# PSUM as one set of eight banks, and small elementwise work given a choice of engine, in a fused attention and channel-mix kernel

## The chip, the cores and the metric

The kernel runs on one core of a Trainium2 chip. The metric is the device time of one execution in microseconds (us). A run is called slow when it is more than 1.5% above the fastest of the same kernel. Experiments of one batch ran on one chip and share the runs of the kernel before. The batches ran on three chips; between batches only ratios are compared.

## The reference

Eight batches, eight heads, 576 positions, head width 64. First comes attention with a feature map whose exponent is shifted by the largest absolute projection of each row, then a channel mix with shifted tokens:

```python
def phi(x):
    proj = np.einsum('bhsd,df->bhsf', x, w_phi)
    proj = proj - np.max(np.abs(proj), axis=-1, keepdims=True)
    return np.concatenate([np.exp(proj), np.exp(-proj)], axis=-1)
q_p, k_p = (phi(q), phi(k))
kv = np.einsum('bhsf,bhsd->bhfd', k_p, v)
num = np.einsum('bhsf,bhfd->bhsd', q_p, kv)
den = np.einsum('bhsf,bhf->bhs', q_p, k_p.sum(axis=2))[..., None] + 1e-06
x = num / den                        # then heads side by side: [8, 576, 512]
# channel mix; x_prev is x shifted by one position
xk = mu_k * x + (1.0 - mu_k) * x_prev
xr = mu_r * x + (1.0 - mu_r) * x_prev
k = np.maximum(xk @ w_k, 0.0)        # 512 -> 1024
v = k * k @ w_v                      # 1024 -> 512
out = 1.0 / (1.0 + np.exp(-(xr @ w_r))) * v
```

## The kernel before

The program is a fixed list of some 1,460 small steps. Each word of the list names a step, after a colon the PSUM place it takes, and after a slash the engine that does it. The steps are recorded in this order, each engine's own among them, and the recording layer puts a semaphore wait wherever two instructions on different engines use the same tile.

```python
ORDER = """
...
xf4/ACT xe4/DVE kc5/ACT h0.0:0 h0.1:1 qb5 rl0.0/ACT rl0.1/ACT sq0.0/ACT vc6/POOL vc7/DVE rk6 qp7:1
...
"""
```

PSUM is cut into three pairs of banks (`P`) and two single banks (`M`). Each use asks the pool for a new tile under the tag of its place:

```python
psum = ctx.enter_context(tc.tile_pool(name="psum", bufs=1, space=bass.MemoryType.PSUM))

def ptile(key, name):
    return psum.tile([128, 2, 512], FP, name=name, tag=f"P{plan.place[key]}")

def motile(key, name):
    return psum.tile([128, 512], FP, name=name, tag=f"M{plan.place[key]}")
```

The matmuls of the channel mix use the singles in turn. A half of `h` goes to one bank while the ReLU (`krelu`) of the other bank is read by ScalarE or VectorE:

```python
def h(fc):
    def f():
        s[fc] = ps = motile(("mo", f"h{b}.{fc}"), "ps_h")
        ...
        for c in range(NDC):
            nc.tensor.matmul(ps, lhsT=wk_bf[:, c, fc * 128:(fc + 1) * 128],
                             rhs=xkt[bp][:, c, m0:m0 + 512], start=(c == 0), stop=(c == NDC - 1))
    return f

def rl(fc):
    def f(eng):
        relu(eng, s["kr", fc], s[fc])
    return f
```

Each maximum is split into a high and a low bf16 part on GpSimd, the two mixes of a channel block are single instructions on VectorE, and GpSimd also issues the input loads:

```python
def mhx():
    nmv = s["nm"].rearrange("p k (a g) -> p k a g", a=2)
    nc.gpsimd.tensor_copy(mhv[:, :, 0], nmv)
    nc.gpsimd.tensor_tensor(mhv[:, :, 1], nmv, mhv[:, :, 0], op=ALU.subtract)
...
def mix(i):
    def f():
        ...
        nc.vector.scalar_tensor_tensor(out=t[:, a, (b % 2) * S:(b % 2 + 1) * S], in0=s["d"],
                                       scalar=mu[:, a:a + 1], in1=xs[:, a, 0:S],
                                       op0=ALU.mult, op1=ALU.add)
    return f
...
def ld(which):
    def f():
        t = get(nat, b, inp, [128, NP, 2 * X], BF, "nat")
        src, o = ((k, 0), (q, X))[which]
        nc.gpsimd.dma_start(out=t[:, a0:a1, o:o + X], in_=heads(src, b, a0, a1))
    return f
```

## Time and profile before

| | before |
|---|---|
| median of 3 runs | 305.4 us (305.16 to 306.32) |
| span of the profiled run | 304.2 us |
| busy: TensorE, VectorE, ScalarE, GpSimd | 278.4, 240.3, 223.3, 127.4 us |
| start of the channel mix of batches 0 to 3 | 51.9, 82.7, 117.4, 153.5 us |
| start-to-start time of TensorE beyond its columns, in gaps over 0.25 us | 24.3 us |

The last row is worked out from the trace: for each pair of neighbouring matmuls, the time between their starts less the time of the first one's columns (at 216 ns for 512 columns, the median in this trace), summed where it is over 250 ns.

A profile line is read from left to right. In the page's map of 40 equal slices each digit is the busy share of a slice in tenths. This is TensorE before:

```profile
PE   6688798999899999969999997999999999999993
```

The start is half empty, there is one dent in the middle, and the rest is 9. In the timeline a line has its start, its length, engine, source line, operation and count; square brackets hold the engine's idle time before it and who ended it. This is the loop of the channel mix before, in the trace's PE view and its VectorE and ScalarE neighbours:

```profile
59.39 1.89 PE L779 MATMUL ps_h<-xk,wk_bf 128*128 128x512 bf16 x8
61.00 0.62 ACT L203 ACTIVATE krelu<-ps_h 128x512 bf16<-128x512 f32 x1
```

Eight matmuls, two halves of `h`, run as one block with no bracket: the second half does not wait for the ReLU of the first.

### The profile page before, as it was taken

To read this page: it belongs to the slowest core of one execution; us is meant where nothing else is said; L and a number is where in the kernel's file an instruction comes from. 1 tells how busy PE (TensorE), PEld (TensorE's weight loads), DVE (VectorE), ACT (ScalarE), POOL (GpSimd) and SP (SyncE) were. 2 spreads that over 40 slices of the span, in tenths; PEclk is the share of its full clock that TensorE was granted. 3 is DMA by queue.
4 is the path that set the end of the run, shared out by engine and by line. 5 is a ranking of instruction groups with operands and counts; after the bars stand their busy time and mean duration, and the time that the engine had idled before them with its cause. 6 is when DMAs were issued, how large, how long until landed. Compare 5 with 4: busy or idle time off the path is not lost.

```text
span 304.2 us, 9054 instructions
## 1 busy us (share of the span) xinstructions
PE 278.4 (92%) x3765; PEld 158.4 (52%) x3813; DVE 240.3 (79%) x369; ACT 223.3 (73%) x408; POOL 127.4 (42%) x261
## 2 busy tenths in 40 slices
PE   6688798999899999969999997999999999999993
PEld 2456465565456655534555654454556655554541
DVE  5776789979978999667978988799869888777331
ACT  3397899998689897855888884898797878923410
POOL 7763533696047346653443714353034403400400
PEclk9999989999999999998999999999999999999999
DMA  8999957399989957996957898913924364233125
GB/s 152 204 209 207 169 83 105 59 194 206 194 174 128 148 124 131 197 200 113 177 110 107 145 125 157 162 47 61 187 60 69 11 93 94 58 74 71 39 58 116
DMA packets 66137, 38.18 MB, mean 126 GB/s; under 512 B 47024, under 2 KB 60720, under 8 KB 66096
## 3 DMA queue, kind: packets, MB, share of 16 engines
q1 hardware_dynamic: 51280, 20.82, 39.4%
q0 software_dynamic: 14672, 16.48, 35.1%
q8 instruction: 30, 0.49, 0.7%
q10 hardware_dynamic: 144, 0.29, 0.3%
q14 instruction: 11, 0.09, 0.1%
HBM read 33.62 MB, written 9.44 MB: 142 GB/s over the span
## 4 chain that ended last, share of the span: by engine, by line
PE 61%; DVE 18%; DMA 7%; ACT 6%; issue 3%; POOL 2%; SPq 1%; DVEq 0%; POOLq 0%
PE ps_v L812 14%; PE ps_h L779 13%; PE ps_r L798 7%; PE ps_nd L656 5%; DMA xs<-x_sc 4%; PE ps_kv L635 4%; DVE nm L565 4%; DVE nm L560 3%; DVE xk L706 2%; PE ps_ve L896 2%; ACT q L620 2%; PE ps_he L866 2%; DVE xr L706 2%; PE ps_q L548 2%; PE ps_k L598 2%
## 5 line engine op out<-in xcount | busy, mean ns | idle before, releaser
L620 ACT ACTIVATE q<-ps_qT 128x512 bf16<-128x512 f32 x128 | 67.1, 622 | 3.0 <-PE ps_qT L612 2.8
L575 ACT ACTIVATE k<-ps_k 128x1024 bf16<-128x1024 f32 x64 | 62.9, 1038 | 5.6 <-PE ps_k L598 4.3
L779 PE MATMUL ps_h<-xk,wk_bf 128*128 128x512 bf16 x237 | 60.8, 379 | 1.3 <-issue 0.3
L812 PE MATMUL ps_v<-wv_bf,kk 128*128 128x512 bf16 x243 | 58.2, 379 | 1.0 <-issue 0.3
L565 DVE TENSOR_REDUCE nm<-ps_q 128x8 f32<-128x1024 f32 x32 | 38.7, 1218 | 4.3 <-PE ps_q L548 4.1
L560 DVE TENSOR_REDUCE nm<-ps_k 128x8 f32<-128x1024 f32 x32 | 38.8, 1217 | 3.8 <-PE ps_k L548 3.8
L812 PEld LDWEIGHTS <-kk 128*128 128x128 bf16 x256 | 23.9, 98 | 28.8 <-issue 1.9
L211 POOL TENSOR_TENSOR kk<-krelu 128x512 bf16<-128x512 bf16 x23 | 23.9, 1047 | 35.4 <-DVE krelu L205 21.7
L779 PEld LDWEIGHTS <-wk_bf 128*128 128x128 bf16 x256 | 22.5, 97 | 25.2 <-issue 2.3
L584 POOL CAST mhl<-nm 128x16 bf16<-128x16 f32 x32 | 8.0, 250 | 64.1 <-DVE nm L560 64.0
L798 PE MATMUL ps_r<-wr_bf,xr 128*128 128x512 bf16 x118 | 32.9, 394 | 1.2 <-issue 0.5
L804 ACT ACTIVATE rt<-ps_r 128x512 bf16<-128x512 f32 x32 | 19.5, 609 | 18.0 <-PE ps_r L798 15.7
L700 POOL TENSOR_TENSOR diff<-xs 128x576 bf16<-128x576 bf16 x21 | 28.0, 1336 | 7.6 <-DVE xs L682 2.8
L203 ACT ACTIVATE krelu<-ps_h 128x512 bf16<-128x512 f32 x39 | 23.2, 611 | 10.1 <-PE ps_h L779 8.3
L706 DVE SCALAR_TENSOR_TENSOR xk<-diff,mu_k_t,xs 128x576 bf16<-128x576 bf16 x32 | 28.5, 892 | 1.3 <-POOL diff L700 1.0
L818 DVE SCALAR_TENSOR_TENSOR ob<-rt,ps_v 128x512 f32<-128x512 bf16 x32 | 21.8, 682 | 8.7 <-PE ps_v L812 4.2
L666 DVE TENSOR_TENSOR x_sc<-ps_nd,rden 128x640 bf16<-128x640 f32 x32 | 26.4, 825 | 1.1
L706 DVE SCALAR_TENSOR_TENSOR xr<-diff,mu_r_t,xs 128x576 bf16<-128x576 bf16 x32 | 26.9, 840 | 0.0
L548 PEld LDWEIGHTS <-qkT 64*128 64x128 bf16 x512 | 17.6, 94 | 12.0 <-issue 9.7
L635 PE MATMUL ps_kv<-v,k 64*128 64x65 bf16 x1024 | 22.8, 192 | 0.6 <-ACT q L620 0.4
L635 PEld LDWEIGHTS <-k 64*128 64x128 bf16 x1024 | 19.9, 95 | 5.1 <-issue 3.8
L205 DVE TENSOR_SCALAR krelu<-ps_h 128x512 bf16<-128x512 f32 x25 | 17.1, 688 | 6.6 <-PE ps_h L779 6.0
(99 smaller groups left out, 467.5 us busy)
## 6 DMA issues: line engine op xcount, KB each, us to landing
out_dram<-ob SPq DMA_DIRECT2D x72, 128.0 KB, 2.4
nat<-in_k_dram POOLq DMA_DIRECT2D x6, 576.0 KB, 8.6
nat<-in_q_dram POOLq DMA_DIRECT2D x6, 576.0 KB, 8.9
vt<-in_v_dram POOLq DMA_DIRECT2D x6, 576.0 KB, 9.6
wk_bf<-in_moe_w_k_dram POOLq DMA_DIRECT2D x2, 512.0 KB, 10.8
wv_bf<-in_moe_w_v_dram POOLq DMA_DIRECT2D x2, 512.0 KB, 12.3
nat<-in_k_dram POOLq DMA_DIRECT2D x3, 288.0 KB, 7.4
nat<-in_q_dram POOLq DMA_DIRECT2D x3, 288.0 KB, 7.3
```

What stands on the lines that cost most here:

```text
L211: (nc.vector if eng == "DVE" else nc.gpsimd).tensor_tensor(out_, in_, in_, op=ALU.mult)
L560: nc.vector.tensor_reduce(s["nm"][:, 0, :], s["k"].rearrange("p a (g f) -> p (a g) f", f=128), axis=AX.X, op=ALU.max, apply_absolute_value ...
L565: nc.vector.tensor_reduce(s["nm"][:, 1, :], s["q"].rearrange("p a (g f) -> p (a g) f", f=128), axis=AX.X, op=ALU.max, apply_absolute_value ...
L575: nc.scalar.activation(s[f"k{pn}"], s["k"].rearrange("p a (g f) -> p (a g) f", f=128), AF.Exp, scale=(1.0 if pn == 0 else -1.0))
L620: nc.scalar.activation(t[:, h, :].rearrange("f (g a p) -> f g a p", g=4, a=2), s["qT"].rearrange("f a (g h p) -> f h g a p", g=4, h=2)[:, ...
L635: nc.tensor.matmul(ps[:, hh, pn * 65:(pn + 1) * 65], lhsT=s[f"k{pn}"][r, c, :], rhs=vb[r, a, 2 * g + par, :], start=(pn == 0 and c == 0), ...
L666: nc.vector.tensor_tensor(s["x"].rearrange("p (b s) d -> p b s d", b=2), ndv[:, :, :, 0:64], s["rd"].to_broadcast([128, 2, 5, 64]), op=ALU ...
L700: (nc.vector if eng == "DVE" else nc.gpsimd).tensor_tensor(s["d"], xs[:, a, 64:64 + S], xs[:, a, 0:S], op=ALU.subtract)
L706: nc.vector.scalar_tensor_tensor(out=t[:, a, (b % 2) * S:(b % 2 + 1) * S], in0=s["d"], scalar=mu[:, a:a + 1], in1=xs[:, a, 0:S], op0=ALU.m ...
L779: nc.tensor.matmul(ps, lhsT=wk_bf[:, c, fc * 128:(fc + 1) * 128], rhs=xkt[bp][:, c, m0:m0 + 512], start=(c == 0), stop=(c == NDC - 1))
L798: nc.tensor.matmul(ps, lhsT=xrt[bp][:, c, m0 + ci * 128:m0 + (ci + 1) * 128], rhs=wr_bf[:, c, :], start=(c == 0), stop=(c == NDC - 1))
L812: nc.tensor.matmul(ps, lhsT=s["kk"][:, fc, ci * 128:(ci + 1) * 128], rhs=wv_bf[:, fc, :], start=(fc == 0), stop=(fc == NFC - 1))
```

## The change

The intent: let any step take any of the eight banks, as a pair or single, so that a fourth pair may be in flight; let an edge tile (the positions beyond 512) use the second bank of its own pair in place of two singles; and let mixes and splits of maxima run on GpSimd or VectorE. The whole list of steps was made anew for this, with 26 of 32 pair splits and 8 of 10 edge splits on VectorE, and 31 of 64 mixes on GpSimd. The core of the diff, with the new list and repetitions cut:

```diff
+    def pick(eng):
+        return nc.vector if eng == "DVE" else nc.gpsimd
...
+    banks = [psum.tile([128, 2, 512], FP, name=f"banks{i}") for i in range(4)]
+
     def fill(n, i):
-        t = psum.tile([128, 512], FP, name="ps_f", tag=f"M{i}")
         for _ in range(n):
-            nc.tensor.matmul(t, lhsT=ones[:, 0:128], rhs=ones, start=True, stop=True)
-    def ptile(key, name):
-        return psum.tile([128, 2, 512], FP, name=name, tag=f"P{plan.place[key]}")
-    def motile(key, name):
-        return psum.tile([128, 512], FP, name=name, tag=f"M{plan.place[key]}")
+            nc.tensor.matmul(banks[i // 2][:, i % 2, :], lhsT=ones[:, 0:128], rhs=ones, start=True, stop=True)
+    def ptile(key):
+        return banks[plan.place[key] // 2]
+    def motile(key):
+        i = plan.place[key]
+        return banks[i // 2][:, i % 2, :]
...
         def mte():
-            s["pm"] = pm = motile(("mo", "m" + tag), "ps_me")
-            nc.tensor.transpose(pm[:, 0:64].bitcast(BF), mh, ident)
+            nc.tensor.transpose(s["ps"][:, 1, 0:64].bitcast(BF), mh, ident)
...
-        def mhx():
+        def mhx(eng):
             nmv = s["nm"].rearrange("p k (a g) -> p k a g", a=2)
-            nc.gpsimd.tensor_copy(mhv[:, :, 0], nmv)
-            nc.gpsimd.tensor_tensor(mhv[:, :, 1], nmv, mhv[:, :, 0], op=ALU.subtract)
+            pick(eng).tensor_copy(mhv[:, :, 0], nmv)
+            pick(eng).tensor_tensor(mhv[:, :, 1], nmv, mhv[:, :, 0], op=ALU.subtract)
...
         def mix(i):
-            def f():
+            def f(eng):
...
+                if eng == "DVE":
+                    nc.vector.scalar_tensor_tensor(out=out_, in0=s["d"], scalar=mu[:, a:a + 1], in1=prev,
+                                                   op0=ALU.mult, op1=ALU.add)
+                else:
+                    md = small.tile([128, S], FP, name="md", bufs=2)
+                    nc.gpsimd.tensor_scalar(md, s["d"], mu[:, a:a + 1], None, op0=ALU.mult)
+                    nc.gpsimd.tensor_tensor(out_, md, prev, op=ALU.add)
```

## The prediction

> **What bounds the kernel now.** I read the shares first, then the stretches, then TensorE's waits, then the timeline of the worst hole. The page's first part:
>
> ```profile
> PE 278.4 (92%) x3765; PEld 158.4 (52%) x3813; DVE 240.3 (79%) x369; ACT 223.3 (73%) x408; POOL 127.4 (42%) x261
> ```
>
> TensorE is the fullest engine, but VectorE and ScalarE are near it, so a small delay on any of the three shows. Modelled ends make 278 too much, so I counted TensorE's real work. From the chain of waits, full-speed pieces: 4 matmuls of 512 columns take 0.86 to 0.87 us, 8 take 1.73, the 20 of one ps_nd 0.64, one ps_he half 0.89; likewise about 2.36 us for all seven groups of one head pair. Sum: channel mix 64x0.865 + 32x0.865 + 32x1.73 + edges 17.5 = 156; pairs 32x2.36 = 75.5; first transposes and edge tiles 15. That is **246 us** plus 39 filler matmuls. The other 58 us of the 304.2 us span are where anything can be won. Where they lie, by stretches cut at the first ps_h of each batch (51.9, 82.7, 117.4, 153.5, ... us; columns as the view heads them: PE, PEld, DVE, ACT, POOL busy, clock, DMA share, GB/s):
>
> ```profile
> 0.00:52.00 52.00, 40.60 (x674) 25.83 (x680) 38.96 (x75) 38.03 (x74) 28.60 (x64) 0.97 1.00 164
> 83.00:117.00 34.00, 33.42 (x537) 20.51 (x544) 30.98 (x44) 28.93 (x54) 16.48 (x36) 1.00 0.96 149
> 117.00:153.50 36.50, 33.18 (x448) 17.77 (x448) 28.62 (x39) 25.89 (x45) 18.73 (x36) 0.95 0.99 162
> 220.00:251.00 31.00, 30.74 (x470) 18.28 (x474) 25.46 (x41) 25.39 (x46) 10.01 (x21) 1.00 0.41 57
> 276.70:304.20 27.50, 22.43 (x124) 10.80 (x124) 9.26 (x16) 7.71 (x13) 3.18 (x3) 0.97 0.36 77
> ```
>
> The start takes 52 us for some 22 us of useful TensorE work: about 30 lost. The last matmul ends near 299.3; 4.9 us are the last eviction and store. In between, 247.4 us hold 224 us of work: 23 lost. So three pots: **30 (start), 23 (middle), 5 (end)**. What TensorE waits for by name:
>
> ```profile
> PE ps_me L476 <- POOL mhlt L471: 3.5, 3, 2.4
> PE ps_m L589 <- DVE ob L818: 1.6, 1, 1.6
> PE ps_e L455 <- ACT qkT L197: 1.4, 1, 1.4
> PE ps_q L548 <- ACT qkT L197: 1.4, 2, 1.0
> PE ps_k L548 <- DVE nm L565: 1.2, 4, 0.3
> PE ps_m L589 <- POOL mhl L585: 1.0, 3, 0.4
> ```
>
> The transposes of the maxima (ps_m, ps_me) head the list: they wait for GpSimd's split of each maximum into two bf16 parts. The longest hole in the timeline shows why GpSimd is late:
>
> ```profile
> 131.54 0.23 POOL L199 COPY xs<-xs 128x63 bf16<-128x63 bf16 x1 [2.80 <-DMA xs<-x_sc]
> ...
> 133.37 0.70 POOL L471 TENSOR_TENSOR mhlt<-me,mhlt 128x4 bf16<-128x4 f32 x1
> ...
> 134.53 0.23 PE L476 MATMUL ps_me<-ident,mhlt 128*128 128x128 bf16 x1 [2.44 <-POOL mhlt L471]
> ...
> 138.55 0.23 POOL L199 COPY xs<-xs 128x63 bf16<-128x63 bf16 x1 [2.48 <-DMA xs<-x_sc]
> ...
> 139.31 0.23 PE L589 MATMUL ps_m<-ident,mhl 128*128 128x128 bf16 x1 [0.27 <-POOL mhl L585]
> ```
>
> GpSimd, which takes its work in order, waits for a DMA transpose[...] (the chain puts 13.4 us on it); the tiny splits stand behind that copy, and TensorE stands behind the splits. Start-to-start gaps of TensorE over 250 ns sum to 3.9 us in 130 to 140, and 12 us in all after 50 us.
>
> [...] 1.6 us of ps_m waits for ps_v's eviction (they share one bank) and 1.2 us of ps_k for the reduction that empties ps_q. [...] the difference of 576 columns has a mean of 1336 ns on GpSimd and 495 on VectorE, 2.7x. [...] the mixes have a median of 814 ns, but one took 1900.
>
> **The change part by part.**
>
> *Order.* The whole order is new: 1462 entries, every bank and engine chosen again; filler falls from 39 to 22. What precedes the first ps_h hardly changes: 7 kp, 5 nd. I multiplied the entries of each order by the durations above. Up to the mix that releases the first channel mix (xb3): VectorE 42.9 before, 43.7 after; ScalarE 39.9 and 40.4; TensorE 22.4 and 23.4. After the last ps_nd (nd31) both have the same 31 us of matmuls. Hence neither end becomes shorter by having less work.
>
> *Maximum splits.* 26 of 32 pairs and 8 of 10 edges move to VectorE. GpSimd loses 26x0.487 + 8x0.85 = 19.5 us. VectorE gains, with small VectorE operations of 0.14 to 0.17 us as a guide (an estimate), 26x0.3 + 8x0.56 = 12.3. The split now follows its reduction on the same engine. In the hole above all splits concerned are on VectorE, and the waiting GpSimd copies have no matmul behind them.
>
> *Mixes.* 15 xa and 16 xb move to GpSimd as two instructions (multiply into f32, then add). Estimate: like its one-input copy, 0.74, plus like its difference, 1.34: 2.1 us each, +65 us; VectorE loses 31x0.87 = 27.
>
> *Squares and copies.* ScalarE takes 13 more squares (+8) and gives up 14 copies of kv and mT (-4.5); GpSimd loses 7 squares (-7) and 5 v copies (-4). With the rest: VectorE about 228, ScalarE 229, GpSimd 162 us. Balanced, and none over TensorE. More overlap with GpSimd stretches VectorE: today some 0.08 us for each two-input operation, if doubled over the 100 left about +8. The relief is then about 5 us of 240: not where the gain is.
>
> *Banks.* A fourth pair may be in flight, and an edge tile takes one pair instead of a pair and two singles. In the built programs TensorE's waits fall from 531 to 420; waits on its own engine, which came with handing a tile over, fall from 102 to 1. VectorE's rise from 295 to 381.
>
> *Sum.* Middle: 3.9 us of the hole goes; of the other 8 us of gaps I give 3 to the banks and the shorter path of the maxima. Start: a fourth pair and splits without the trip over GpSimd take 2 of the 30, since the work before xb3 is unchanged (filler there fills idle time, so 17 fewer give nothing). End: 0. Together -9: 305.4 - 9 = **296.5 us**.
>
> **The rivals.**
> 1. *Same holes elsewhere* (300 to 306). The lost middle time is DMA transposes late among loads; a new order meets them at another place. For it: DMA share is near 1 up to 150 us, and every batch still needs its transposes. Against: the matmuls behind are no longer tied to GpSimd.
> 2. *GpSimd[...] becomes the bound* (303 to 310). A chain transpose, copy, difference, two mixes on GpSimd lasts 0.35+1.3+4.2 = 5.9 us against 2.5 on VectorE; four pairs make 23 us of the 31 us of a batch[...]. For it: the 1900 ns mix. Against: only half the mixes move, and the last batch mixes on VectorE.
> 3. *The freedom does more* (285 to 292). A fourth pair lets ScalarE and VectorE, each idle 13 to 14 us in the start, run ahead; the start falls to 46 and the middle loses 12 instead of 23.
>
> **Range and chances.** The floor is 22 + 224 + 5 plus a start that data and ScalarE's 40 us do not let go under about 45, so about 275 to 280; today is 304. I put the centre at one third of the way, 296.5, the range from rival 3 to the mild form of rival 1: 289 to 304. Faster by over 2% means under 299.3. The centre is 3 us below that: chance 0.66; same 0.31; slower, which needs rival 2 in full, 0.03.
>
> **What would show it.** Right: first ps_h at 49 to 51 us; no TensorE gap above 2 us; ps_m and ps_me waiting on GpSimd for under 1 us; VectorE busy 225 to 240, ScalarE 225 to 235, GpSimd 155 to 175; a GpSimd mix of about 2.1 us in all; middle loss near 16. Wrong: a GpSimd wait ahead of ps_h (late mixes), mixes or splits on VectorE stretched well beyond 0.9 and 0.3 us, or a new hole of several us with the clock falling to 0.83[...].

## The result

The changed kernel is correct and takes 361.7 us (median of 4, 360.5 to 363.4) against 305.4 us (305.2 to 306.3) beside it. A ratio in this document is the mean time of one kernel's fast runs over that of the kernel before in the same rounds, so not quite the ratio of the medians quoted; here it is 1.184, 95% interval 1.179 to 1.189. It is **slower by 18%**, and the prediction of 296.5 us was wrong.

The part on shares in the page after, and TensorE's slices:

```profile
PE 288.8 (81%) x3796; PEld 162.4 (45%) x3796; DVE 240.7 (67%) x432; ACT 230.7 (64%) x411; POOL 191.8 (53%) x226
...
PE   7867689878778968687887786897977998989893
```

TensorE, VectorE and ScalarE have within 4% of the work that they had, and their shares have fallen by 9 to 12 points; GpSimd has more work, but stands idle for nearly half of the span. Nobody became the bound; all wait more. TensorE's 9s are gone from one end to the other, so the loss is not one hole. By stretches from one batch's channel mix to the next (the columns are stretch, length, busy time of PE, PEld, DVE, ACT and POOL with their instructions, clock, DMA share, GB/s), first before, batches 0 and 1, then after:

```profile
51.90:82.70 30.80, 29.38 (x383) 16.31 (x385) 27.39 (x40) 26.17 (x49) 17.67 (x29) 1.00 0.95 153
82.70:117.40 34.70, 34.12 (x546) 20.82 (x550) 31.45 (x45) 29.19 (x55) 16.88 (x36) 1.00 0.95 150
```

```profile
54.30:89.10 34.80, 28.86 (x379) 15.56 (x377) 26.52 (x48) 25.07 (x48) 19.79 (x15) 1.00 0.49 85
89.10:141.90 52.80, 42.09 (x594) 24.47 (x592) 34.28 (x60) 33.87 (x60) 30.32 (x35) 0.94 0.77 127
```

The first channel mix starts only 2.5 us later than before (54.4 against 51.9); the loss comes after it, 4 us in batch 0, 18 in batch 1 and some 30 in the later ones. TensorE's gaps over 0.25 us sum to 80.0 us, 55.7 more than before, which is the whole loss of 56 us. The granted clock is lower too, 0.971 in the mean of this run against 0.986; an estimate of the time lost to it, (1 - clock) x span, is 10.4 us against 4.2, so at most some 6 us of the loss can be that. TensorE's waits by name (line that waited, who ended it, us in total, times, longest), the first of them:

```profile
PE banks L792 <- DVE krelu L212: 7.6, 9, 1.5
PE banks L792 <- ACT krelu L210: 7.3, 6, 2.7
PE banks L597 <- DVE mhl L593: 4.7, 4, 2.5
```

L792 is the first matmul of the channel mix. Before, it had 1.3 us of idle time ahead of it in the whole run. Now it waits for ReLUs, and the timeline shows which. The list of steps puts three halves of `h` at banks 6, 7 and 6 (`h0.5:6 h0.6:7 h0.7:6`), with their ReLUs on VectorE, ScalarE and ScalarE:

```profile
65.50 0.68 DVE L212 TENSOR_SCALAR krelu<-banks 128x512 bf16<-128x512 f32 x1
66.23 1.02 PE L792 MATMUL banks<-xk,wk_bf 128*128 128x512 bf16 x4 [0.82 <-DVE krelu L212]
67.29 0.60 ACT L210 ACTIVATE krelu<-banks 128x512 bf16<-128x512 f32 x1 [0.47 <-PE banks L792]
67.94 1.02 PE L792 MATMUL banks<-xk,wk_bf 128*128 128x512 bf16 x4 [0.69 <-ACT krelu L210]
```

The matmuls of 66.23 go to bank 7, and wait until VectorE has read bank 6. Those of 67.94 go to bank 6, which has been free since 66.18, and wait until ScalarE has read bank 7. Matmul and reader take turns where before they overlapped. Banks 6 and 7 are one tile.

I then went through the waits of the built programs and looked, for each, at what the instruction that waits and the one waited for have in common. **False waits**, where the two touch the same tile but different banks or parts of it, number 9 before and 172 after: 87 of TensorE on a reader, 32 of a reader on TensorE, the rest of readers on readers. (These are counts of the program as it was built, not of the trace.) The trace names some of the last kind too:

```profile
DVE krelu L212 <- ACT krelu L210: 7.6, 5, 2.9
ACT rt L817 <- DVE ob L831: 7.0, 3, 4.9
```

The other two costs that the prediction put numbers on were also larger. First GpSimd by shapes after (shapes, count, busy us, mean ns, then the idle time), then VectorE's splits:

```profile
L720 POOL TENSOR_SCALAR md<-diff,mu_r_t 128x576 f32<-128x576 bf16 x16 | 28.8, 1801 | 10.2 <-DVE diff L708 10.0
L721 POOL TENSOR_TENSOR xr<-md,xs 128x576 bf16<-128x576 f32 x16 | 20.6, 1290 | 1.3
```

```profile
L593 DVE TENSOR_TENSOR mhl<-nm,mhl 128x16 bf16<-128x16 f32 x26 | 9.4, 361 | 0.9
L592 DVE CAST mhl<-nm 128x16 bf16<-128x16 f32 x26 | 8.1, 312 | 0.9
```

A mix on GpSimd takes 1.8 + 1.3 = 3.1 us, not 2.1, and a split on VectorE 0.67 us, not 0.3.

### The profile page after: what moved, and what is told of

Its sections match the earlier page's. It is cut to its first block, busy times and chain, and to the rows that moved or that the text cites. A ratio compares the mean times of both kernels' runs of the same rounds, so it can differ in the third digit from the quotient of the medians.

```text
span 358.7 us, 9134 instructions
## 1 busy us (share of the span) xinstructions
PE 288.8 (81%) x3796; PEld 162.4 (45%) x3796; DVE 240.7 (67%) x432; ACT 230.7 (64%) x411; POOL 191.8 (53%) x226
## 4 chain that ended last, share of the span: by engine, by line
PE 47%; DVE 24%; ACT 18%; issue 5%; DMA 2%; POOL 2%; SPq 0%; DVEq 0%; ACTq 0%; POOLq 0%
PE banks L825 13%; PE banks L792 11%; PE banks L811 6%; ACT krelu L210 5%; DVE krelu L212 4%; ACT q L628 3%; DVE ob L831 3%; DVE nm L568 3%; DVE nm L573 3%; ACT rt L817 3%; ACT k L583 2%; PE banks L664 2%; PE banks L879 2%; PE banks L643 2%; PE banks L556 2%
## 5 line engine op out<-in xcount | busy, mean ns | idle before, releaser
L792 PE MATMUL banks<-xk,wk_bf 128*128 128x512 bf16 x256 | 64.0, 384 | 18.7 <-DVE krelu L212 7.6
L628 ACT ACTIVATE q<-banks 128x512 bf16<-128x512 f32 x128 | 66.4, 608 | 12.5 <-PE banks L620 12.4
L583 ACT ACTIVATE k<-banks 128x1024 bf16<-128x1024 f32 x64 | 62.5, 1031 | 10.4 <-PE banks L606 10.1
L825 PE MATMUL banks<-wv_bf,kk 128*128 128x512 bf16 x256 | 59.9, 379 | 4.5 <-ACT rt L817 3.0
L792 PEld LDWEIGHTS <-wk_bf 128*128 128x128 bf16 x256 | 24.0, 98 | 47.5 <-issue 24.1
L573 DVE TENSOR_REDUCE nm<-banks 128x8 f32<-128x1024 f32 x32 | 38.7, 1219 | 9.5 <-PE banks L556 9.5
L568 DVE TENSOR_REDUCE nm<-banks 128x8 f32<-128x1024 f32 x32 | 39.0, 1219 | 5.5 <-PE banks L556 4.6
L811 PE MATMUL banks<-wr_bf,xr 128*128 128x512 bf16 x128 | 33.4, 389 | 9.8 <-ACT krelu L210 3.9
L720 POOL TENSOR_SCALAR md<-diff,mu_r_t 128x576 f32<-128x576 bf16 x16 | 28.8, 1801 | 10.2 <-DVE diff L708 10.0
L556 PE MATMUL banks<-wph,qkT 64*128 64x128 bf16 x512 | 25.9, 224 | 4.7 <-DVE x_sc L674 3.0
L720 POOL TENSOR_SCALAR md<-diff,mu_k_t 128x576 f32<-128x576 bf16 x15 | 26.4, 1762 | 5.4 <-DVE diff L708 4.3
L674 DVE TENSOR_TENSOR x_sc<-banks,rden 128x640 bf16<-128x640 f32 x32 | 26.4, 825 | 1.1
L556 PEld LDWEIGHTS <-qkT 64*128 64x128 bf16 x512 | 18.0, 98 | 12.3 <-issue 10.2
```

The lines of the kernel that those rows point to most:

```text
L556: nc.tensor.matmul(ps[:, par, g * 128:(g + 1) * 128], lhsT=qkT[b][r, g0 + gg + g, :], rhs=wph[r, :], start=(g == 0), stop=(g == 3))
L568: nc.vector.tensor_reduce(s["nm"][:, 0, :], s["k"].rearrange("p a (g f) -> p (a g) f", f=128), axis=AX.X, op=ALU.max, apply_absolute_value ...
L573: nc.vector.tensor_reduce(s["nm"][:, 1, :], s["q"].rearrange("p a (g f) -> p (a g) f", f=128), axis=AX.X, op=ALU.max, apply_absolute_value ...
L583: nc.scalar.activation(s[f"k{pn}"], s["k"].rearrange("p a (g f) -> p (a g) f", f=128), AF.Exp, scale=(1.0 if pn == 0 else -1.0))
L628: nc.scalar.activation(t[:, h, :].rearrange("f (g a p) -> f g a p", g=4, a=2), s["qT"].rearrange("f a (g h p) -> f h g a p", g=4, h=2)[:, ...
L720: nc.gpsimd.tensor_scalar(md, s["d"], mu[:, a:a + 1], None, op0=ALU.mult)
```

## The experiments

The theory (A): the halves of one tile are ordered as if they were one buffer, and this alone serializes TensorE with the readers. The rivals: (B, C) the mixes on GpSimd, by their own time or by stretching VectorE's operations beside them (before, one of VectorE's mixes took 1900 ns beside GpSimd's difference and copy, where the median is 814); (D) static tiles in place of tiles handed out per use; (E, F) the new order of steps itself.

### 1. The false waits, taken away and put in

**a_nodep**: the changed kernel, with every ordering declared absent where two instructions on different engines touch different banks of a tile and have no other tile in common.

```diff
+    def split_banks(new):
+        for b in new:
+            ob = others(b)                         # tiles other than banks
+            for m, bk in banks_of(b).items():      # tile -> banks touched
+                for a, abk, aob in hist.setdefault(m, []):
+                    if a.engine != b.engine and not (bk & abk) and not (ob & aob):
+                        tc.declare_no_dep(b, a, reason="other bank")
+                hist[m].append((b, bk, ob))
```

> The changed kernel, same order, same instructions, same banks; only the dependencies between two instructions of different engines that touch different banks of one two-bank PSUM tile (and share nothing else) are declared absent. Theory A (the two halves of one tile are ordered as if they were one buffer: in the built program 87 waits of TensorE on a reader of the other bank, 32 of readers on a writer of the other bank, 51 of readers on readers): 290 to 305 us, near the 296.5 of the prediction, and no TensorE wait for a krelu ahead of ps_h. Rival B (mixes on GpSimd, 3.06 us each where 2.1 were assumed) and rival C (the new order is simply worse): 345 to 362 us, unchanged.

Measured: 323.1 us (median of 4, 319.1 to 328.0), against 306.7 beside it. Two of the four runs were slow by the rule above, so there is no interval; its two fast runs give a ratio of 320.4 / 306.5 = 1.045. The false waits in the built program fall from 172 to 4, and the waits of L792 on ReLUs leave the head of the list. So A accounts for some 14 of the 18 points, about 42 us on fast runs (38.5 on all). My range of 290 to 305 was missed by 18 us all the same: something else costs 14 to 17 us. TensorE's first two waits now:

```profile
PE banks L597 <- DVE mhl L593: 10.2, 9, 3.4
PE banks L556 <- DVE x_sc L674: 5.5, 2, 5.0
```

**n_peonly**: the same, with only the false waits of TensorE taken away.

```diff
-                    if a.engine != b.engine and not (bk & abk) and not (ob & aob):
+                    if a.engine != b.engine and "PE" in str(b.engine) and not (bk & abk) and not (ob & aob):
```

> The changed kernel with only TensorE's 87 false waits taken away, and the false waits of VectorE, ScalarE and GpSimd on the other half of a tile left in. Theory A-PE (TensorE's own waits on readers of the other half are what costs): 320 to 332 us, nearly all of the 38.5 us. Rival A-readers (the readers that queue behind one another are as much to blame, and TensorE then waits for the late reader of its own bank): 338 to 358 us.

Measured: 332.5 us, ratio 1.085 [1.078, 1.092], a hair above the expected range. TensorE's own 87 false waits are 9.9 of the 13.9 points; those of the readers are the other 4, in this order of taking them away; the readers' alone were not taken away.

**b_shared**: the other direction. The kernel before, its order and engines unchanged, with the two singles as halves of one tile. **b_split**: the same static tiles, but the two singles are two tiles.

```diff
+    ptiles = [psum.tile([128, 2, 512], FP, name=f"ppair{i}") for i in range(3)]
+    mpair = psum.tile([128, 2, 512], FP, name="mpair")        # b_split: two tiles [128, 512]
+    mtiles = [mpair[:, i, :] for i in range(2)]
     def ptile(key, name):
-        return psum.tile([128, 2, 512], FP, name=name, tag=f"P{plan.place[key]}")
+        return ptiles[plan.place[key]]
     def motile(key, name):
-        return psum.tile([128, 512], FP, name=name, tag=f"M{plan.place[key]}")
+        return mtiles[plan.place[key]]
```

> The kernel before with its own order, engines and banks; the three pairs and the two single banks become tiles that live for the whole kernel, and the two single banks are the halves of one tile, as in the changed kernel. Theory A: the false waits alone make it slow, 330 to 370 us, with TensorE waiting for krelu and rt of the other single bank. Rivals B and C: nothing that they name has changed, 304 to 308 us.

> As b_shared, but the two single banks are two tiles. Separates the shared tile from the fact that tiles live for the whole kernel and are no longer handed over by a pool. Theory A: 303 to 309 us, as before. If tiles that live for the whole kernel are themselves the cost: near b_shared.

Measured: b_shared 401.6 us, ratio 1.309 [1.303, 1.315]; b_split 306.4 us, ratio 0.999 [0.995, 1.004]. One shared tile costs 95 us in the order made for two, more than I had expected and more than the change itself; static tiles cost nothing, and D is out. TensorE's waits in b_shared are again those on readers of the other half:

```profile
PE mpair L781 <- ACT krelu L203: 8.1, 11, 1.4
PE mpair L781 <- DVE krelu L205: 6.6, 8, 1.9
```

The built programs hold the sharpest lesson. Counting TensorE's waits whose other side I could tell: 518 before, 417 in b_split, **385 in b_shared** and 393 in the changed kernel. The kernel with the fewest waits is the slowest of the four.

**bs_nodep**: b_shared with the false waits between its halves declared absent (the edit of a_nodep on `mpair`).

> The kernel before with its two single banks as halves of one tile (which took 401.6 us), and now the orderings between instructions that touch different halves declared absent. Theory A (the 95 us were nothing but false waits between the two halves): back to the time before, 304 to 309 us. Rival D (sharing a tile costs by something else too, such as the way its address is formed or the waits are placed): it stays above 315 us.

Measured: 306.1 us, ratio 0.998 [0.993, 1.002]. All 95 us were false waits. The shared tile costs nothing else.

### 2. The mixes on GpSimd

**a_dvemix**: the changed kernel with its 31 mixes back on VectorE. **n_dvemix**: the same on top of a_nodep.

```diff
-tp1.0:4 qt3:0 qa3 nd2:6 rt1.0 mhe1.0/DVE mte1.0+1@2 mce1.0/ACT kp4:2 xb0/POOL qb3 rd2 qte1.0 eqe1.0
+tp1.0:4 qt3:0 qa3 nd2:6 rt1.0 mhe1.0/DVE mte1.0+1@2 mce1.0/ACT kp4:2 xb0/DVE qb3 rd2 qte1.0 eqe1.0
...
```

> The changed kernel with all 31 mixes of GpSimd back on VectorE, same order and banks. Theory A: VectorE gets 27 us more work but is not the bound, 352 to 368 us. Rival B (GpSimd mixes are the cost): 310 to 330 us. Rival C: 355 to 365 us.

> a_nodep (false waits gone, 323 us) with all 31 GpSimd mixes back on VectorE, same order. Theory A2 (of the 17 us that a_nodep is still over before, most comes from the mixes on GpSimd: 3.0 us each, and VectorE's maximum splits standing behind them, up to 1.27 us for an operation that takes 0.17 alone): 302 to 312 us, mhl operations on VectorE with a mean under 0.25 us, TensorE's wait for mhl on VectorE under 5 us. Theory C2 (the order itself is worse): 318 to 332 us, because VectorE gains 27 us of work in an order that was not made for it.

Measured: a_dvemix 367.2 us, ratio 1.196 [1.190, 1.202]: with the false waits in place the mixes are not the cause, and moving them back makes it slightly worse. n_dvemix 314.3 us, ratio 1.023 [1.014, 1.033] (one of its runs was slow): without the false waits the mixes are worth about 2 points, some 7 us. Neither of the expected ranges, 302 to 312 and 318 to 332, was hit; the truth lies between.

How the mixes cost time is seen in a_nodep. The timeline at 79 us, lines of other steps left out:

```profile
79.50 1.27 POOL L721 TENSOR_TENSOR xk<-md,xs 128x576 bf16<-128x576 f32 x1
79.57 1.23 DVE L593 TENSOR_TENSOR mhl<-nm,mhl 128x16 bf16<-128x16 f32 x1
...
80.86 0.23 PE L597 MATMUL banks<-ident,mhl 128*128 128x128 bf16 x1 [3.39 <-DVE mhl L593]
```

The low part of the maximum, 16 columns, takes 1.23 us and ends with GpSimd's addition beside it (at 80.80 and 80.77 us), and TensorE stands behind it. Over the whole of a_nodep the same operation has (minimum, median, maximum in ns):

```profile
L593 DVE TENSOR_TENSOR mhl<-nm,mhl x26: 174/176/1267, 13.0 to 274.9; 128x16 bf16<-128x16 f32 x26
```

The maximum is about the length of GpSimd's addition (1271 to 1297 ns). In n_dvemix the maximum falls to 702 ns, and TensorE's waits for this line from 10.2 to 4.5 us.

**n_mdbf**: a_nodep with the product of a mix kept in bf16, to see why the multiply takes 1.72 us rather than the 0.74 of a copy.

```diff
-                    md = small.tile([128, S], FP, name="md", bufs=2)
+                    md = small.tile([128, S], BF, name="md", bufs=2)
```

> The changed kernel without its false waits (323.1 us), with the product of each mix kept in bf16 rather than f32 on the way. Theory C1 (GpSimd's multiply takes 1.72 us because it writes 4-byte results): the multiply falls below 1.2 us, GpSimd's busy time by over 12 us, and the time to 314 to 320 us. Theory C2 (the multiply costs the same whatever it writes): 1.7 us and 321 to 326 us as before. Precision only is lost by it.

Measured: 319.9 us, ratio 1.043 [1.037, 1.049], as a_nodep's fast runs (so the time alone, just inside C1's range, says nothing for C1). The multiply did not get shorter, and the output type is not the reason:

```profile
L720 POOL TENSOR_SCALAR md<-diff,mu_r_t 128x576 bf16<-128x576 bf16 x16 | 29.0, 1811 | 1.4 <-DVE diff L708 1.2
```

### 3. The splits of maxima

**n_poolmh**: a_nodep with all splits back on GpSimd. **n_both**: with splits on GpSimd and mixes on VectorE, so with the engines of the kernel before.

```diff
-rq0 pb1/ACT eqe0.0 kp0:0 ekt0.0 pa1/ACT rk0 lv1.0.d:0 mh0/DVE pt2:2+3@2 pa2/ACT wr.1.d:0 pb2/DVE tr2
+rq0 pb1/ACT eqe0.0 kp0:0 ekt0.0 pa1/ACT rk0 lv1.0.d:0 mh0/POOL pt2:2+3@2 pa2/ACT wr.1.d:0 pb2/DVE tr2
...
```

> a_nodep with the 26 pair splits and 8 edge splits back on GpSimd, mixes stay on GpSimd. If it is the splits' place on VectorE (blocked by GpSimd) that costs, this is faster than 323: 310 to 318. If GpSimd's queue is the trouble (mixes of 3 us ahead of a split in order), it is slower: 325 to 345 us, TensorE waiting for mhl on GpSimd for over 20 us. I expect the latter.

> a_nodep with splits back on GpSimd and mixes back on VectorE: the engines of the kernel before in the order and on the banks of the changed one. Against n_dvemix it gives the worth of the split's move without GpSimd mixes. If the splits gain on VectorE: n_dvemix is 3 to 6 us faster than this. Expected 305 to 318 us.

Measured, as ratios, with the false waits gone in all four:

| | mixes partly on GpSimd | all mixes on VectorE |
|---|---|---|
| most splits on VectorE | 1.045 (a_nodep, 2 fast runs) | 1.023 (n_dvemix) |
| all splits on GpSimd | 1.184 (n_poolmh, 363.3 us) | 1.116 (n_both, 342.9 us) |

Both runs were slower than I expected (325 to 345, and 305 to 318). The order was made for splits on VectorE, where a split follows its reduction; on GpSimd it queues, behind mixes of 3 us or behind loads (n_both's longest wait, 7.7 us at 18 us, ends with a split that stands behind eight loads issued from 7.8 to 17.4 us). TensorE's waits in n_poolmh:

```profile
PE banks L597 <- POOL mhl L593: 36.5, 14, 8.5
PE banks L485 <- POOL mhlt L481: 17.9, 5, 7.7
```

n_both is the clearest sign that **an order does not carry over to other engines**: its engines for splits and mixes are those of the kernel before, it has no false waits, and it is 11.6% slower.

**b_dvemh**: the kernel before with all splits on VectorE, order unchanged.

```diff
-            nc.gpsimd.tensor_copy(mhv[:, :, 0], nmv)
-            nc.gpsimd.tensor_tensor(mhv[:, :, 1], nmv, mhv[:, :, 0], op=ALU.subtract)
+            nc.vector.tensor_copy(mhv[:, :, 0], nmv)
+            nc.vector.tensor_tensor(mhv[:, :, 1], nmv, mhv[:, :, 0], op=ALU.subtract)
```

> The kernel before with all maximum splits (pairs and edges) on VectorE, nothing else changed. The prediction gave the hole at 130 to 140 us (3.9 us) and part of 3 us more to this part. If so: 299 to 303 us, no gap of TensorE over 2 us near 131 us. If the splits merely wait elsewhere (behind other VectorE work, or blocked by GpSimd): 304 to 309 us.

Measured: 318.1 us, ratio 1.037 [1.030, 1.044], against both expectations. The hole at 131 us is gone, but in the place of one long wait on GpSimd there are many short ones on VectorE:

```profile
PE ps_m L589 <- DVE mhl L585: 6.4, 10, 1.7
PE ps_me L476 <- DVE mhlt L471: 3.1, 6, 0.9
```

These two come to 9.5 us, against 4.5 us on the same lines and GpSimd before; the rest of the 11.3 us is not named.

**b_hole**: the kernel before, with only the three splits of that hole on VectorE.

```diff
-tp4.0:0 kv15:1 kc15/ACT h2.6:0 sq2.4/ACT rl2.5/DVE rt4.0 mhe4.0 rl2.6/DVE nd14:1 rd14 h2.7:1 qb15
+tp4.0:0 kv15:1 kc15/ACT h2.6:0 sq2.4/ACT rl2.5/DVE rt4.0 mhe4.0/DVE rl2.6/DVE nd14:1 rd14 h2.7:1 qb15
...
```

(and `mh16/DVE`, `mh17/DVE` in the next lines)

> The kernel before with just three of its splits of maxima (the 16th and 17th of the main rows and the extra one of the fourth batch, those of the hole at 130 to 140 us) on VectorE in place of GpSimd. My predicted step (the hole is worth 3.9 us, and comes from these splits standing behind other work on GpSimd): 301.5 to 304 us. Rival (the next wait comes soon after it, or the later buffers set the pace anyway): 304.5 to 306.5 us.

Measured: 303.95 us against 306.4, ratio 0.991 [0.988, 0.995] in 5 rounds. This is the one version that **beats both kernels**, by 0.9% or 2.7 us; the interval leaves out 1. The stretch of the hole, before and then in b_hole:

```profile
125.00:145.00 20.00, 16.91 (x220) 8.69 (x222) 14.72 (x21) 12.53 (x22) 11.03 (x24) 0.91 1.02 158
```

```profile
125.00:145.00 20.00, 17.50 (x237) 9.29 (x231) 18.19 (x31) 14.23 (x25) 10.62 (x19) 1.00 1.05 175
```

TensorE is busy longer, the clock stays at 1.00 where it was 0.91, and more gets done (237 matmuls against 220). The gaps in 130 to 140 us fall from 3.9 to 2.8 us; the largest, 1.67 us, now ends with a ReLU on ScalarE. That is 1.1 us of the 2.7. The clock differs as well, over all fast runs of the batch: 0.994 in the mean against 0.987, and (1 - clock) x span, again an estimate, falls from 3.9 to 1.9 us. Whether the shorter hole brought the better clock is not shown.

### 4. What is left of the new order

With the false waits gone 4.5 points stay. **n_norar** takes away from a_nodep also the orderings between two engines that only read one bank; **n_close** does that to n_dvemix, so that all three suspects are gone; **n_load** moves in n_close five input loads ahead of two squarings that GpSimd stands before.

```diff
-                    if a.engine != b.engine and not (bk & abk) and not (ob & aob):
+                    if a.engine != b.engine and not (ob & aob) and (not (bk & abk) or (rd and ard)):
```

```diff
-vc8/DVE r0.0:7 th0.0 ka7 rl0.5/DVE nd6:4 ea7 eb7 rd6 h0.6:7 rl0.6/ACT sq0.4/POOL h0.7:6 rl0.7/ACT
+vc8/DVE r0.0:7 th0.0 ka7 rl0.5/DVE nd6:4 ea7 eb7 rd6 h0.6:7 rl0.6/ACT lk3.0 lq3.0 lv3.0 sq0.4/POOL h0.7:6 rl0.7/ACT
...
```

(with `lk3.0 lq3.0 lv3.0` taken out of their later places, and `lk4.0 lq4.0` moved ahead of `sq1.0/POOL` in the same way)

> The changed kernel without its false waits (323.1 us), and now also without the orderings between two engines that both only read one bank. Theory A3 (readers queue behind readers of the same bank, and this is part of the 17 us still missing): 312 to 319 us. Rival (only the mixes on GpSimd and the order are left as causes): 320 to 326 us.

> The changed kernel without its false waits, without the orderings between two readers of one bank, and with its 31 mixes on VectorE: all three causes taken away at once. If they add up (38.5 + 9 + 5.6 us off 361.7): 306 to 311 us, and nothing is left for the new order itself. Rival (the new order, made for other loads, costs by itself): 312 us or more.

> The kernel with all three causes taken away (314.9 us), with five input loads (third and fourth batch) moved ahead of the two squarings that GpSimd stands before. Theory E (the new order's late loads are what is left): 306 to 311 us, and the third batch's feed-forward starts at 117 to 121 us in place of 125.8. Rival F (the loads are early enough, and what is left is spread over the order of VectorE's and TensorE's work): 313 to 317 us.

Measured: n_norar 317.5 us, ratio 1.031 [1.024, 1.038]; n_close 314.9 us, 1.030 [1.024, 1.035]; n_load 312.9 us, 1.021 [1.017, 1.026].

n_norar looks like 1.4 points less than a_nodep's two fast runs, but n_close is no better than n_dvemix (1.023). The two don't add up, and I call the waits among readers **inconclusive**. The waits concerned are between readers of successive uses of a bank. These three kernels are for measurement and no version to keep: what happens when ScalarE and VectorE read one bank at the same time, no run here shows. In a_nodep, n_norar and n_close I laid the bank of each of the 362 reads of ScalarE and 258 of VectorE beside its times in the trace, and no two overlapped on a bank. Against a cost of such waits speaks b_split: its built program has 180 waits between ScalarE and VectorE where before has 123, at a ratio of 0.999; but that is the old order. The kernels a_nodep, n_dvemix and bs_nodep keep every ordering within a bank.

The expectation that n_close would return to 306 to 311 us failed. Its trace showed why loads are late. GpSimd in n_close, its two squarings and the loads of K and V of batch 3, then the same two loads before:

```profile
62.72 1.04 POOL L218 TENSOR_TENSOR kk<-krelu 128x512 bf16<-128x512 bf16 x1 [18.23 <-DVE krelu L212]
63.70 0.81 POOL L326 DMA_DIRECT2D nat<-in_k_dram  x1
...
85.08 1.63 POOL L218 TENSOR_TENSOR kk<-krelu 128x512 bf16<-128x512 bf16 x1 [11.44 <-ACT krelu L210]
86.66 0.81 POOL L331 DMA_DIRECT2D vt<-in_v_dram  x1
```

```profile
61.59 0.79 POOL L316 DMA_DIRECT2D nat<-in_k_dram  x1
...
63.10 0.76 POOL L321 DMA_DIRECT2D vt<-in_v_dram  x1
```

(Batches are counted from 0: the "third and fourth batch" of the expectation are 3 and 4, and the channel mix that starts at 125.8 us is that of batch 2.) GpSimd takes its queue in order, and a squaring that waits 18.2 us for its ReLU holds up the loads behind it. The first load is only 2 us later than before; V of batch 3 and the two loads of batch 4 behind it are some 24 us later. In one slice of n_close the transfers are at 2 GB/s. n_load issues the first of the five at 43.3 us rather than 63.7 and V of batch 3 at 53.4 rather than 86.7, and gains 2.0 us on the medians, though the two intervals just meet. The channel mix of batch 2 starts at 124.3 us in place of 125.8, not at the 117 to 121 that theory E asked for. So E is a part at most, as far as this run tests it: the loads of batch 4 are still at 73.5 and 74.3 us where before has 63.8 and 64.6, and one slice is still at 2 GB/s. The last 2.1 points, some 6.5 us, are spread: TensorE's gaps sum to 37.5 us in n_load against 24.3 before, no wait by name is over 3.8 us in total, and **their cause stays open**.

## Why the prediction was wrong

**The step that failed is "Banks".** It read the built programs: TensorE's waits fall from 531 to 420, those on its own engine from 102 to 1, a fourth pair may be in flight; and it entered this as a gain inside the 3 us given to "the banks and the shorter path of the maxima". What the runs showed in its place:

- The waits that vanished were worth nothing. b_split removes the same 101 handover waits and has a ratio of 0.999.
- Behind the falling count stood 172 waits of a new kind, between banks that have nothing to do with each other. They cost about 42 us of 56. a_nodep shows it by taking them away, b_shared by putting 220 of them into the kernel before, and bs_nodep by taking those away again.
- The diff held the cause in plain sight: `banks[i // 2][:, i % 2, :]` in place of a tile for each bank. I read the change as eight free banks. In its tiles it is four buffers of two banks.
- I saw that VectorE's waits rise from 295 to 381 and did not ask on what. Counted in the built programs by what they wait for, those on VectorE itself rise from 54 to 135, and those on ScalarE, which hold the readers' false waits, from 54 to 97.

**Two terms of the sum were mis-sized, and they close the busy times.** The mix on GpSimd was set at 2.1 us and is 3.1: the multiply is 1.8 us where I took a copy's 0.74. For 31 mixes 95 us in place of 65, and GpSimd is at 191.8 us where I said 162. A split on VectorE was set at 0.3 us and is 0.67 in the mean. Its two operations have medians of 175 and 176 ns, but took up to 785 and 1237, and these longest ones end with an addition of GpSimd (50.94 and 50.90 us, 85.08 and 85.04). With the edges that makes 23.9 us in place of 12.3, and VectorE is at 240.7 where I said about 228. ScalarE at 230.7 is as predicted (229).

**"Maximum splits" was right in its mechanism only.** The hole comes from splits behind other work on GpSimd: in b_hole it shrinks, and the kernel gains 2.7 us of the predicted 3.9, part of which may be the clock. But I gave the move of 34 splits the hole's gain and no cost. Moved in the old order they cost 11.3 us (b_dvemh), as they then stand behind other work on VectorE.

**"Start" and "End".** The first channel mix was to start at 49 to 51 us; it starts at 54.4, and in a_nodep at 52.5, no earlier than before. The fourth pair gives no lead that any run shows.

**"Order"** was entered at no cost. With everything else taken away 2.1 points stay (n_load), and why is open.

**The rivals.** Rival 2 held the right second-order costs (the mix chain, and VectorE's operations stretched, as in its mix of 1900 ns), but as the whole cause it is refuted by a_dvemix: 367.2 us. It accounts for about 2 of 18 points, and only once the false waits are gone. Rival 3 did not occur, and rival 1 was too mild. None of the three had "a wait takes the place of the one removed" between PSUM banks, and so the chance of slower stood at 0.03. Of the signs of being wrong that the prediction named, one came: splits on VectorE took 0.67 us, well beyond 0.3. The others, a hole of several us with a falling clock and a late GpSimd ahead of `h`, were not what came: the loss lies in many waits of up to 2.7 us, at a mean clock of 0.971. One reading of the prediction was also a little high: TensorE's gaps after 50 us sum to 11 us in a recount, not 12.

**The account**, in ratios to the kernel before:

| kernel | ratio | what is gone |
|---|---|---|
| changed | 1.184 | |
| n_peonly | 1.085 | TensorE's false waits |
| a_nodep | 1.045 (2 fast runs) | all false waits |
| n_dvemix | 1.023 | and mixes on GpSimd |
| n_load | 1.021 | and reader orderings, late loads |
| before | 1 | the new order itself: open |

## What to carry to other kernels

Ask of any buffer what the unit of ordering is: here two halves of one tile that different engines use in turn were one buffer (ratio 1.309 in b_shared, 0.998 in bs_nodep with the ordering declared absent), so give each bank that is handed over by itself a tile of its own, or declare the ordering absent and check for races. Do not count waits; for each kind of wait that a change adds, ask which bytes the two sides share. And move a small operation to another engine only at the places where the profile shows it late: three splits moved gained 0.9%, all of them moved lost 3.7%.

## Times of single operations

- A multiply of 576 columns by a scalar of each partition has a median of 1724 ns on GpSimd (a_nodep), slower than the two-input addition there (1276 ns) and 2.6 times the copy of as many columns (667 ns before, where VectorE's copy takes 449); a bf16 result in place of f32 changes nothing (1722 ns, n_mdbf).
- The difference of 576 columns had a mean of 1336 ns on GpSimd and 495 on VectorE before, 2.7 times.
- A VectorE operation with a median of 176 ns took up to 1267 ns in a_nodep, about the length of GpSimd's addition beside it.
